# First batch of an attention and two-layer kernel: transposing the exponentials on TensorE in float32 instead of by DMA, and a new rule for VectorE or GpSimd

## The chip, the cores and the metric

One core of a Trainium2 chip. The metric is the time of one execution on the device, in microseconds; the lower, the better.

## What is computed

The input is q, k and v of 2 batches, 8 heads, 576 positions and 64 features, and the weights of two feed-forward blocks; all is float32.

```python
q_rot, k_rot = rotate(q), rotate(k)                      # rotary embedding
scores = q_rot @ k_rot^T / 8                             # per batch and head, 576 x 576
E = exp(scores - rowmax); attn = E / (rowsum(E) + 1e-9)
x = (attn @ v), heads side by side                       # 1152 tokens x 512
x = ((x @ w_a) * (x @ w_b)) @ w_out                      # 512 -> 1536 -> 512
h = x @ w_in; out = (h * tanh(softplus(h))) @ w_out2     # 512 -> 2048 -> 512
```

## The kernel before

The kernel doesn't issue instructions as it is written. Each call on an engine is recorded with a priority (`at(t)` sets it) in a `Plan`; `Plan.order` (from line 284) then places all operations with costs of its own (`Plan.cost`) and `issue` (line 376) emits them in that order, each engine's queue in order. All instructions are therefore traced at line 388, and the names of tiles tell them apart. Calls on `any_` may go to VectorE or GpSimd: GpSimd takes one if its end is at most SLACK after VectorE's, VectorE only if it ends at least BIAS earlier (lines 37 and 38).

Attention is cut into 72 units of 128 query rows (`UNITS`), 9 for each pair of heads: four row blocks for each of the two heads and one "rest" unit that holds the last 64 rows of both. Units 0 to 35 are the first batch. `attend(n)` does one:

- TensorE writes the scores into a PSUM tile s, 128x576 in two halves, with the key in two parts (qk and kl). q and k come in with the features on the partitions, and `rope` rotates them, a pair of heads ahead (products qkr and kl on `any_`, qk on ScalarE and VectorE).
- VectorE takes the negative row maximum m; ScalarE takes the exponential in place in PSUM.
- ScalarE casts it to float16 (the high part of pp), VectorE subtracts to get the low part (also pp).
- One transposing DMA on SyncE's queue turns pp (128 x 1152 float16) into pt, nine 128x128 blocks, since 576 + 576 columns are 4.5 blocks each.
- TensorE multiplies the blocks with the value parts vhl (high and low) and, for the low part of E, the shifted copy vh: 14 matmuls, into o. A first column of ones gives the row sum.
- `finish` inverts the row sums (den) and scales o into xn on VectorE for every second unit; for a rest unit into xbd. `transpose_x` brings xn and xbd onto the other axis (tile xt) with TensorE and splits it into x.

Layer 1 of the first batch (l from x and w) and layer 2 (l from ab and w) are recorded with priorities among the units of the second batch; then come layers 1 and 2 of the second batch, then the last two products (h, acc). `weights` loads a packed weight tile wr, VectorE decodes it with three integer instructions into xw, it is kept in DRAM for later (ka, ko, kc, read back as wc), ScalarE rounds it to the first part of w and an `any_` subtraction makes the second part. Layer 1 makes a_sb and ab, the latter's second part also by an `any_` subtraction. In the last stage `hidden` evaluates h into g and `accumulate` adds up acc.

PSUM holds 3 s tiles (two banks each) and 2 o tiles in the first batch, then 2 s, 2 o and 2 l.

```python
SLACK = 2000
BIAS = 2500
OFF = dict(S=-4, M=-2, E=-2, P=0, T=-1, V=4, N=-2, X=-4)   # priority offsets of a unit's steps
```

Of the kernel before, what the change touches and what calls it, by code (L numbers as in the profile page):

```python
# [9 lines left out]
F32 = mybir.dt.float32  # L10
F32R = mybir.dt.float32r
F16 = mybir.dt.float16
# [21 lines left out]
START = dict(pe=1144, sp=550)  # L34
BASE = BYTES.__array_interface__["data"][0]
TICK = 3413
SLACK = 2000
BIAS = 2500
FSLACK = 1000
FBIAS = 0  # L40
MARGIN = 0
# [129 lines left out]
class Plan:  # L171
# [88 lines left out]
    def cost(self, key, method, out, args, kw, views):  # L260

        if key == "sp":
            v = views[0]
            if method == "dma_start_transpose":
                return 1356, 1008
            return 475, int(np.prod(v.a.shape)) * v.a.itemsize / 360
        psum = any(v.root.pool.space == PSUM for v in views if v is not out)
        n = max(v.n for v in views)
        pointers = sum(v.n == 1 for v in views if v is not out) if out.n > 1 or method == "tensor_scalar" else 0
        if key == "pe":  # L270
            rhs = kw["rhs"] if method == "matmul" else args[1]
            n = rhs.n
            return n * (2 if rhs.root.dtype == F32 else 1), n * rhs.a.shape[0] / 128
        if key == "act":
            return n / 1.2 + (51 if psum else 93) + 93 * min(pointers, 1), 0
        if key == "dve":
            fast = method.startswith("tensor_scalar") or method == "tensor_copy"
            if psum:
                return n / 0.96 + 65 + 58 * min(pointers, 1), 0
            return n / (1.92 if fast else 0.96) + 69 + 58 * min(pointers, 1), 0  # L280
        if key == "pool":
            return (n * 2.132 + 132 if method != "memset" else n), 0

    def order(self):
# [17 lines left out]
        while True:  # L302
# [46 lines left out]
            if e == "sp":  # L349
                tr = op.call[1] == "dma_start_transpose"  # L350
                d0 = max(dma_free, start + (1300 if tr else 1100))
                dma_free = d0 + op.dma
                if tr:
                    free[e] = dma_free - 952
                op.end = dma_free
            else:
                op.end = free[e]
# [92 lines left out]
def kernel(ctx: ExitStack, tc: tile.TileContext, qk, v5, w1, w2, w34, tab, out):  # L450
# [13 lines left out]
    def open_pool(name, bufs=1, side="left", space=None):  # L464
        kw = dict(name=name, bufs=bufs)
        if space is not None:
            kw["space"] = space
        if space != bass.MemoryType.DRAM:
            kw.update(side=side, reuse_waits="tile")
        p = Pool(plan, space, kw)  # L470
        return p, p

    def close_pool(p):
        p.close()
# [5 lines left out]
    a0_cm, a0_p = open_pool("att0")  # L480
    d_cm, d_p = open_pool("kept", space=bass.MemoryType.DRAM)
    a_cm, a_p = open_pool("att", side="right")
    o_cm, o_ps = open_pool("o_ps", 2, side="right", space=PSUM)
    s_cm, s_ps = open_pool("s_ps", 3, space=PSUM)

    def at(t):

        plan.prio = 1000 * t
# [55 lines left out]
    xbd = [a_p.tile([128, 128], F32, tag=f"xbd{i}", name=f"xbd{i}") for i in range(2)]  # L544
    vhl = [(a_p if i < 2 else a0_p).tile([128, 5, 2, 130], F16, tag=f"vhl{i}", name=f"vhl{i}") for i in range(3)]

    vh2 = [(a_p if i < 2 else a0_p).tile([128, 4, 2, 66], F16, tag=f"vh2{i}", name=f"vh2{i}") for i in range(3)]
    vb = (0, 1, 2, 0, 1, 0, 1, 0)
    istk = ident[:, 128:192]

# [75 lines left out]
    def v_split(p):  # L626
        of = vhl[vb[p]].rearrange("p c h e -> p (c h) e")
        vt, up = v_t[p].rearrange("p (n d) -> p n d", d=D), v_up[:, p : p + 1]
        hi = of[:, :, 1 : D + 1]
        act.activation(hi, vt, AF.Copy, scale=up)  # L630
        dve.scalar_tensor_tensor(of[:, :, D + 1 : 2 * D + 1], vt, up, hi, op0=ALU.mult, op1=ALU.subtract)
        v, v2 = vhl[vb[p]], vh2[vb[p]]
        sp.dma_start(v2[0:64], v[64:128, 0:4, :, 0:66])
        sp.dma_start(v2[64:128], v[0:64, 1:5, :, 0:66])
        sp.dma_start(v[64:128, 4, :, 0 : 2 * D + 1], v[0:64, 0, :, 0 : 2 * D + 1])


    def ring_tile(n, shape, dtype, tag):
        first = n < NU // 2
        bufs = {"pp": (6, 3), "pt": (6, 4)}[tag][0 if first else 1]  # L640
        return (a0_p if first else a_p).tile(shape, dtype, tag=tag, name=f"{tag}{n}", bufs=bufs)

    o_t, xn_t, den_t = {}, {}, {}

    def attend(n):
        t0_ = t_unit(n)

        p, h, c = UNITS[n]
        tq, tk = qk_t[p]
        rest = h is None  # L650
        at(t0_ + OFF["S"])
        st = s_ps.tile([128, 2, 512], F32, tag="s", name=f"s{n}")
        for hf in range(2):
            ks = slice(HS * hf, HS * hf + HS)
            ops = []
            for i in (0, 1) if rest else (h,):
                lhsT = qz[p % 2][:, i, :] if rest else tq[i][:, 128 * c : 128 * c + 128]
                ops += [(lhsT, tk[i][:, ks]), (lhsT, kl[p % 2][i][:, ks])]
            for i, (lhsT, rhs) in enumerate(ops):
                pe.matmul(st[:, hf, :HS], lhsT=lhsT, rhs=rhs, start=(i == 0), stop=(i == len(ops) - 1))  # L660

        at(t0_ + OFF["M"])
        m = a_p.tile([128, 1], F32, tag="m", name=f"m{n}", bufs=4)
        e = st[:, :, :HS]
        dve.tensor_reduce(m, e, axis=AX.XY, op=ALU.max, negate=True)
        at(t0_ + OFF["E"])
        act.activation(e, e, AF.Exp, bias=m)
        at(t0_ + OFF["P"])
        pp = ring_tile(n, [128, 2 * S], F16, "pp")
        hi, lo = (pp[:, c : c + S].rearrange("p (a b) -> p a b", a=2) for c in (0, S))  # L670
        act.copy(hi, e)
        dve.tensor_tensor(lo, e, hi, op=ALU.subtract)
        at(t0_ + OFF["T"])
        pt = ring_tile(n, [128, 9, 128], F16, "pt")
        sp.dma_start_transpose(out=pt, in_=pp)

        at(t0_ + OFF["V"])
        vt = vhl[vb[p]]
        if rest or c % 2 == 0:
            o_t[p] = o_ps.tile([128, 512], F32, tag="o", name=f"o{n}")  # L680
        o = o_t[p]
        for i in range(9):
            for lo, w in ((0, D + 1), (D + 1, D)):
                if lo and i >= 5:
                    continue
                oc = 1 if lo else 0
                v = vt[:, i] if i < 5 else vh2[vb[p]][:, i - 5]
                if rest:
                    oo = o[:, 0:132].rearrange("p (a b) -> p a b", a=2)[:, :, oc : oc + w]
                    rhs = v[:, :, lo : lo + w]  # L690
                else:
                    base = 66 * (c % 2) + oc
                    oo = o[:, base : base + w]
                    rhs = v[:, h, lo : lo + w]
                pe.matmul(oo, lhsT=pt[:, i, :], rhs=rhs, start=(i == 0 and lo == 0), stop=(i == 8))
        if rest or c % 2:
            at(t0_ + OFF["N"])
            finish(p, rest, h, c // 2)

    def finish(p, rest, h, g):  # L700

        key = "r" if rest else h
        early = p == SPLIT
        oo = o_t[p][:, 0:132].rearrange("p (a b) -> p a b", a=2)
        den = a_p.tile([128, 2], F32, tag=f"den{key}", name=f"den{p}_{key}_{g}", bufs=2)
        dve.tensor_scalar(den, oo[:, :, 0], 1e-9, v_up[:, p : p + 1], op0=ALU.add, op1=ALU.mult)
        dve.reciprocal(den, den)
        if rest:
            for i in range(2):
                r = slice(64 * i, 64 * i + 64)  # L710
                dve.tensor_scalar_mul(xbd[p % 2][r, r], oo[r, i, 1 : D + 1], den[r, i : i + 1])
            return
        part = early and g
        if (p, part) not in xn_t:
            xp = a0_p if p in (0, 2) or early else a_p
            n = 2 if early else 4
            xn_t[p, part] = xp.tile([128, 4, 2, D], F32, tag="xn", name=f"xn{p}_{g}", bufs=2 if xp is a0_p else 1)[:, 0:n]
        c = 0 if early else 2 * g
        dve.tensor_tensor(
            xn_t[p, part][:, c : c + 2, h, :], oo[:, :, 1 : D + 1], den.unsqueeze(2).to_broadcast([128, 2, D]), op=ALU.mult  # L720
        )

# [142 lines left out]
        pool.memset(xbd[i], 0.0)  # L865
    for i in range(3):
        pool.memset(vhl[i][:, :, :, 0:1], 1.0)
    at(0)

    t = o_ps.tile([128, 512], F32, tag="o", name="warm")  # L870
# [29 lines left out]
    for n in range(NU):  # L900
        p, h, c = UNITS[n]
        if n == NU // 2:
            close_pool(s_cm)
            l_cm, l_ps = open_pool("l_ps", 2, space=PSUM)
            s_cm, s_ps = open_pool("s_ps2", 2, space=PSUM)
        if n == NU // 2 + 2:
            close_pool(a0_cm)
            ab_cm, ab_p = open_pool("ab")
        attend(n)
        if n == V_AT:  # L910
            at(t_unit(n) + VP[2])
            for i in range(1, NP):
# [37 lines left out]
    T = layer1(0, T, DT * G, F0)  # L950
    y0 = layer2(0, T, DT * G, between2)
    T += 24 * DT * G
    close_pool(s_cm)
    close_pool(o_cm)
    close_pool(a_cm)
# [158 lines left out]
```

## Time and profile before

| | us |
|---|---|
| runs, median of 3 | 645.03 (642.63 to 646.7) |
| the profiled execution, whole | 647.88 |
| its span, first to last instruction | 646.1 |
| TensorE busy | 573.7 |
| VectorE busy | 391.8 |
| GpSimd busy | 324.7 |
| ScalarE busy | 309.4 |

PE is TensorE's matmuls, PEld its weight loads, DVE VectorE, ACT ScalarE, POOL GpSimd, SP SyncE. In the stretches, PEclk is the granted TensorE clock as a share of 2.4 GHz: 0.50 is the lower level, 1.2 GHz. A wait is told as who waited, for whom, in total, how often, and the longest.

### The profile page before, as it was taken

The numbers are of one execution on the slowest core, as the hardware profiler recorded it, in microseconds if no ns is written. First come the engines' busy times: TensorE is split into PE (matmuls) and PEld (weight loads), VectorE is DVE, ScalarE is ACT, GpSimd is POOL, SyncE is SP. The second block draws the span as 40 slices with busy tenths as digits, with TensorE's granted clock in tenths as the row PEclk, the third lists the DMA queues.
The fourth block names the chain that finished last, engine by engine and source line by source line (L and its number), as shares of the span: only waits on it lengthen the run. The fifth ranks groups of instructions, "written<-read, shape, count | busy, mean of one in ns | idle before, by whom it ended". The sixth has DMA issues, their size and how long they took to land.

```text
span 646.1 us, 11253 instructions
## 1 busy us (share of the span) xinstructions
PE 573.7 (89%) x4168; PEld 523.6 (81%) x4168; DVE 391.8 (61%) x687; ACT 309.4 (48%) x583; POOL 324.7 (50%) x261
## 2 busy tenths in 40 slices
PE   6575656699899888899999999999999999999997
PEld 5564545589788777788999999997888899899885
DVE  6979768979688877889668999971101112111111
ACT  4957646557465564444344444226443345343230
POOL 5460753465853763423489787557444443332120
PEclk7676767779899988999999999999999999999999
DMA  8496997977878986999799788974333324220002
GB/s 290 87 201 166 218 238 149 209 209 210 200 161 204 274 183 174 230 304 271 209 399 329 238 282 281 293 280 138 112 97 96 89 92 138 80 79 17 1 1 82
DMA packets 135127, 118.13 MB, mean 183 GB/s; under 512 B 99232, under 2 KB 100896, under 8 KB 135072
## 3 DMA queue, kind: packets, MB, share of 16 engines
q1 hardware_dynamic: 135072, 117.41, 66.6%
q8 instruction: 33, 0.54, 0.3%
q14 instruction: 22, 0.18, 0.1%
HBM read 74.61 MB, written 20.19 MB: 147 GB/s over the span
## 4 chain that ended last, share of the span: by engine, by line
PE 67%; DMA 19%; DVE 8%; ACT 3%; issue 2%; SPq 1%; POOL 0%; DVEq 0%; ACTq 0%; POOLq 0%
PE l L388 28%; DMA pt<-pp 16%; PE acc L388 16%; PE h L388 15%; PE o L388 5%; PE s L388 3%; DVE pp L388 2%; DMA wr<-in_w_dram 2%; DVE m L388 1%; DVE xw L388 1%; SPq L388 1%; DMA qkr_k<-in_qk_dram 1%; DVE qk L388 1%; ACT qk L388 1%; PE xt L388 1%
## 5 line engine op out<-in xcount | busy, mean ns | idle before, releaser
L388 POOL TENSOR_TENSOR w<-wc,w 128x512 fp32r<-128x512 f32 x100 | 135.8, 1361 | 146.6 <-ACT w L388 125.5
L388 PE MATMUL l<-x,w 128*128 128x320 f32 (+1 forms) x1152 | 172.9, 305 | 1.5 <-ACT w L388 1.0
L388 PEld LDWEIGHTS l<-x,w 128*128 128x128 f32 x1152 | 161.0, 195 | 2.5 <-ACT w L388 1.5
L388 DVE SCALAR_TENSOR_TENSOR xw<-wr,xw 128x512 uint32<-128x512 uint32 x136 | 128.2, 959 | 0.1
L388 DVE TENSOR_TENSOR g<-h,g 128x320 fp32r<-128x320 f32 (+1 forms) x48 | 26.8, 558 | 155.6 <-ACT g L388 155.6
L388 PE MATMUL acc<-w,g 128*128 128x512 f32 x432 | 105.7, 396 | 0.6 <-ACT g L388 0.6
L388 PE MATMUL h<-y,w 128*128 128x320 f32 (+1 forms) x576 | 104.8, 336 | 0.2 <-DVE g L388 0.2
L388 PEld LDWEIGHTS h<-y,w 128*128 128x128 f32 x576 | 93.5, 188 | 9.7 <-DVE g L388 0.5
L388 ACT CAST w<-wc 128x512 fp32r<-128x512 f32 x100 | 61.4, 619 | 80.7 <-PE l L388 24.5
L388 PEld LDWEIGHTS acc<-w,g 128*128 128x128 f32 x432 | 80.6, 188 | 19.0 <-ACT g L388 1.0
L388 PEld LDWEIGHTS <-pt 128*128 128x128 f16 x1008 | 47.0, 110 | 49.3 <-DMA pt<-pp 41.6
L388 POOL TENSOR_TENSOR w<-xw,w 128x512 fp32r<-128x512 f32 x36 | 49.5, 1378 | 68.0 <-ACT w L388 62.9
L388 PE MATMUL l<-ab,w 128*128 128x256 f32 (+1 forms) x576 | 81.8, 298 | 1.7 <-ACT w L388 1.5
L388 PEld LDWEIGHTS l<-ab,w 128*128 128x128 f32 x576 | 77.5, 190 | 2.9 <-ACT w L388 2.3
L388 PE MATMUL o<-vhl,pt 128*128 128x65 f16 (+1 forms) x720 | 46.4, 216 | 37.4 <-DMA pt<-pp 33.9
L388 ACT ACTIVATE s<-s,m 128x576 f32<-128x576 f32 x72 | 50.8, 715 | 46.8 <-DVE m L388 42.7
L388 POOL TENSOR_TENSOR ab<-a_sb,ab 128x256 fp32r<-128x256 f32 (+1 forms) x48 | 50.7, 1060 | 27.9 <-ACT ab L388 20.1
L388 POOL TENSOR_TENSOR qkr<-qkr,cs 128x576 f32<-128x576 f32 x28 | 41.8, 1510 | 42.6 <-DMA qkr<-in_qk_dram 42.6
L388 PE MATMUL s<-qk 128*128 128x288 f32 x128 | 45.8, 370 | 18.1 <-DVE pp L388 13.2
L388 DVE TENSOR_TENSOR pp<-s,pp 128x576 f16<-128x576 f32 x72 | 53.5, 749 | 11.1 <-ACT pp L388 10.6
L388 DVE TENSOR_SCALAR xw<-wr 128x512 uint32<-128x512 uint32 x68 | 51.7, 774 | 10.0 <-DMA wr<-in_w_dram 8.5
L388 DVE TENSOR_REDUCE m<-s 128x1 f32<-128x576 f32 x72 | 53.1, 749 | 5.3 <-PE s L388 5.0
(73 smaller groups left out, 578.7 us busy)
## 6 DMA issues: line engine op xcount, KB each, us to landing
wr<-in_w_dram SPq DMA_DIRECT2D x68, 512.0 KB, 5.1
wc<-kc SPq DMA_DIRECT2D x64, 256.0 KB, 2.7
kc<-xw SPq DMA_DIRECT2D x32, 256.0 KB, 3.3
qkr<-in_qk_dram SPq DMA_DIRECT2D x14, 576.0 KB, 5.4
ka<-xw SPq DMA_DIRECT2D x24, 256.0 KB, 2.7
wc<-ka SPq DMA_DIRECT2D x24, 256.0 KB, 5.8
ko<-xw SPq DMA_DIRECT2D x12, 256.0 KB, 3.1
wc<-ko SPq DMA_DIRECT2D x12, 256.0 KB, 3.7
```

The lines of the kernel that those rows point to most:

```text
L388: getattr(engine, method)(*map(real, args), **{k: real(v) for k, v in kw.items()})
```

## The change

In the first batch `attend0` takes the place of `attend`. The exponential goes from PSUM to an SBUF tile e (float32, one for two units). TensorE transposes four blocks of 128x128 of each unit into PSUM (tile tm, 512 columns), and for a pair of units their last 128 columns into tile tr (256 columns, 128 for a rest unit). ScalarE casts the transposed PSUM tile to float16 (the high part) and VectorE subtracts (the low part), into ptm and ptr. The fifth block overlaps the fourth, so its value tile vr has zeros in the upper half; all parts use the same value tiles, 15 matmuls a unit. `finish` copies o to SBUF (ob) on ScalarE in the first batch, and scales it into xn on `any_`. PSUM holds 2 s, 1 o, 2 tm and 1 tr in the first batch, then 2 s, 2 o and 2 l. SLACK and BIAS become 0, so that an `any_` operation goes to the engine that would end it first. The planner's costs of a DMA and three offsets of priorities differ too.

```diff
-SLACK = 2000
-BIAS = 2500
+SLACK = 0
+BIAS = 0
...
-                return 1356, 1008
-            return 475, int(np.prod(v.a.shape)) * v.a.itemsize / 360
+                return 1356, 1700
+            return 475, int(np.prod(v.a.shape)) * v.a.itemsize / 320
...
-                    free[e] = dma_free - 952
+                    free[e] = max(free[e], dma_free - 1700)
...
-OFF = dict(S=-4, M=-2, E=-2, P=0, T=-1, V=4, N=-2, X=-4)
+OFF = dict(S=-8, M=-8, E=-8, P=0, T=-1, V=4, N=-2, X=-4)
...
-    o_cm, o_ps = open_pool("o_ps", 2, side="right", space=PSUM)
-    s_cm, s_ps = open_pool("s_ps", 3, space=PSUM)
+    o_cm, o_ps = open_pool("o_ps", 1, side="right", space=PSUM)
+    s_cm, s_ps = open_pool("s_ps", 2, side="right", space=PSUM)
+    t_cm, t_ps = open_pool("t_ps", 1, space=PSUM)
...
+        if p < NP:
+            pool.tensor_copy(vr[vb[p]][64:128, :, 0 : 2 * D + 1], v[64:128, 4, :, 0 : 2 * D + 1])
+            return
...
+    def attend0(n):
...
+        s, m = scores(n)
+        if not j:
+            e_t[0] = a0_p.tile([128, 2, S], F32, tag="e", name=f"e{n}", bufs=3)
+        e = e_t[0]
+        act.activation(e[:, j, :].rearrange("p (a b) -> p a b", a=2), s, AF.Exp, bias=m)
+
+        def parts(x, name, bufs):
+            w = 128 * len(x)
+            at(t0_ + OFF["T"])
+            t = t_ps.tile([128, w], F32, tag=name, name=f"{name}{n}", bufs=bufs)
+            for i, b in enumerate(x):
+                pe.transpose(t[:, 128 * i : 128 * i + 128], b, ident[:, 0:128])
+            at(t0_ + OFF["P"])
+            pt = a0_p.tile([128, 2, w], F16, tag=f"p{name}", name=f"p{name}{n}", bufs=6)
+            act.copy(pt[:, 0, :], t)
+            dve.tensor_tensor(pt[:, 1, :], t, pt[:, 0, :], op=ALU.subtract)
+            return pt
+
+        pt_t[j] = parts([e[:, j, 128 * i : 128 * i + 128] for i in range(4)], "tm", 2)
+        if not (rest or j):
+            return
+        pr = parts([e[:, i, S - 128 :] for i in range(1 + j)], "tr", 1)
+        for i in (0,) if rest else (0, 1):
+            chunks = [(*(pt_t[i][:, q, 128 * k : 128 * k + 128] for q in (0, 1)), vhl[vb[p]][:, k]) for k in range(4)]
+            chunks.append((*(pr[:, q, 128 * i : 128 * i + 128] for q in (0, 1)), vr[vb[p]]))
+            weighted(n if rest else n - 1 + i, chunks)
...
+        if p < NP:
+            ob = a0_p.tile([128, 2, 66], F32, tag="ob", name=f"ob{p}_{key}_{g}", bufs=3)
+            act.copy(ob[:, :, 0 : D + 1], oo[:, :, 0 : D + 1])
+            oo, eng = ob, any_
...
-        attend(n)
+        (attend0 if n < NU // 2 else attend)(n)
```

How the order of the instructions moves is seen at two places. The first is TensorE's queue in the first batch, after scores of the second pair of heads. Before, the output matmuls of a unit (o, here of a rest unit) stand between scores, and each needs the block pt that a DMA brings:

```order
L388 MATMUL s_413<-kl_98,qk_229 128x288
L388 MATMUL s_427<-qk_229 128x288
L388 MATMUL vs_434<-ident,v_mx 3x128
L388 MATMUL s_427<-kl_98,qk_229 128x288
L388 MATMUL s_427<-qk_229 128x288
L388 MATMUL s_427<-kl_98,qk_229 128x288
L388 LDWEIGHTS pt_345
L388 MATMUL o_444<-vhl_128,pt_345 128x2x65
```

Now, in the first pair of heads, transposes of e into tm and tr stand between the scores, and the output matmuls take their weights from ptm and ptr:

```order
L388 MATMUL s_313<-kl_95,qk_169 128x288
L388 MATMUL tm_311<-ident,e_262 128x128 x3
L388 MATMUL tr_328<-ident,e_262 128x128 x2
L388 LDWEIGHTS ptm_257
L388 MATMUL o_338<-vhl_131,ptm_257 128x65
L388 MATMUL tm_340<-ident,e_302 128x128 x4
L388 MATMUL s_347<-qk_169 128x288
L388 MATMUL s_347<-kl_95,qk_169 128x288
```

No instruction of that queue waits for a transposing DMA any more until the second batch; it waits for ScalarE and VectorE instead. The second place is VectorE's queue in the second batch, where weights are decoded (xw) between the maxima (m) and the subtractions (pp) of the units. Before:

```order
L388 SCALAR_TENSOR_TENSOR xw_2698<-wr_2456,xw_2698 128x512
L388 SCALAR_TENSOR_TENSOR xw_2711<-wr_2573,xw_2711 128x512
L388 TENSOR_SCALAR den_1_0_2759<-o_2704,v_up 128x2
L388 TENSOR_TENSOR pp_2706<-s_2653,pp_2706 128x576
L388 RECIPROCAL den_1_0_2759<-den_1_0_2759 128x2
L388 TENSOR_REDUCE m_2774<-s_2683 128x1
```

Now, at the same kind of place:

```order
L388 SCALAR_TENSOR_TENSOR xw_3030<-wr_2737,xw_3030 128x512
L388 TENSOR_REDUCE m_3057<-s_3047 128x1
L388 SCALAR_TENSOR_TENSOR xw_3054<-wr_2868,xw_3054 128x512
L388 TENSOR_TENSOR w_3059<-xw_3030,w_3059 128x512
L388 SCALAR_TENSOR_TENSOR xw_3054<-wr_2868,xw_3054 128x512
L388 TENSOR_TENSOR pp_2963<-s_2898,pp_2963 128x576
L388 TENSOR_SCALAR xw_3086<-wr_2955 128x512
L388 TENSOR_TENSOR w_3079<-xw_3054,w_3079 128x512
```

The subtractions that make the second part of w have come over from GpSimd's queue into VectorE's, among the work of the units.

## Rows read from the trace of the kernel before

**Rows 1.** The page: TensorE's busy time, and the chain by engine and by line.
```profile
PE 573.7 (89%) x4168; PEld 523.6 (81%) x4168; DVE 391.8 (61%) x687; ACT 309.4 (48%) x583; POOL 324.7 (50%) x261
...
PE 67%; DMA 19%; DVE 8%; ACT 3%; issue 2%; SPq 1%; POOL 0%; DVEq 0%; ACTq 0%; POOLq 0%
PE l L388 28%; DMA pt<-pp 16%; PE acc L388 16%; PE h L388 15%; PE o L388 5%; PE s L388 3%; DVE pp L388 2%; DMA wr<-in_w_dram 2%; DVE m L388 1%; DVE xw L388 1%; SPq L388 1%; DMA qkr_k<-in_qk_dram 1%; DVE qk L388 1%; ACT qk L388 1%; PE xt L388 1%
```

**Rows 2.** The maxima m (first and last start); busy time in A, B, C, D.
```profile
L388 DVE TENSOR_REDUCE m<-s x72: 731/748/760, 15.0 to 304.9; 128x1 f32<-128x576 f32 x72
...
core 0: us, PE busy (x) PEld busy (x) DVE busy (x) ACT busy (x) POOL busy (x), PEclk, DMA share, GB/s
...
15.00:136.30 121.30, 76.82 (x716) 67.16 (x717) 97.96 (x197) 75.74 (x127) 58.09 (x40) 0.68 0.87 186
136.30:304.90 168.60, 150.49 (x1366) 140.50 (x1365) 142.54 (x279) 95.67 (x176) 88.80 (x70) 0.97 0.86 218
304.90:440.00 135.10, 135.03 (x1043) 134.55 (x1042) 111.34 (x142) 50.83 (x107) 94.27 (x73) 1.00 0.84 280
440.00:646.10 206.10, 201.53 (x1009) 173.15 (x1007) 30.67 (x54) 80.67 (x161) 76.31 (x60) 1.00 0.27 79
```

**Rows 3.** The chain in order of time: start, us, what; two pieces.
```profile
105.42 0.95 PE o L388 x14
...
317.65 122.40 PE l L388 x916
```

**Rows 4.** TensorE's waits in A: who for whom, us, times, longest.
```profile
PE o L388 <- DMA pt<-pp: 20.6, 17, 3.0
PE s L388 <- DVE pp L388: 12.2, 7, 3.0
```

**Rows 5.** The same in B.
```profile
PE o L388 <- DMA pt<-pp: 13.3, 10, 3.0
```

**Rows 6.** VectorE's timeline near 286 us: start, us, instruction.
```profile
285.92 0.75 DVE L388 TENSOR_TENSOR pp<-s,pp 128x576 f16<-128x576 f32 x1
286.58 0.48 DVE L388 TENSOR_TENSOR y<-l,y 128x320 fp32r<-128x320 f32 x1
```

**Rows 7.** VectorE's groups by shape: times, busy us, mean ns, idle before.
```profile
L388 DVE TENSOR_TENSOR g<-h,g 128x512 fp32r<-128x512 f32 x16 | 11.1, 692 | 66.2 <-ACT g L388 66.2
L388 DVE TENSOR_TENSOR a_sb<-a_sb,l 128x256 f32<-128x256 f32 x24 | 9.9, 414 | 5.6 <-PE l L388 5.5
...
L388 DVE TENSOR_TENSOR xn<-o,den 128x128 f32<-128x128 f32 x32 | 9.0, 281 | 0.0
```

**Rows 8.** Busy time by stretch: VectorE's fullest 50 us.
```profile
350.00:400.00 50.00, 50.00 (x378) 50.00 (x377) 45.98 (x53) 21.48 (x47) 39.90 (x32) 1.00 0.84 275
```

**Rows 9.** Two xt transposes in TensorE's timeline, and the stretch around them.
```profile
174.58 0.63 PE L388 MATMUL xt<-ident,xn 128*128 128x128 f32 x2
175.00 0.53 PE L388 MATMUL xt<-ident,xbd 128*128 128x64 f32 x2
...
174.50:175.20 0.70, 0.70 (x5) 0.70 (x4) 0.00 (x0) 0.00 (x0) 0.70 (x1) 0.50 0.49 105
```

**Rows 10.** VectorE on tiles xw and pp: ns min/median/max; then xw's group (mean ns).
```profile
L388 DVE SCALAR_TENSOR_TENSOR xw<-wr,xw x136: 662/685/1837, 64.0 to 432.4; 128x512 uint32<-128x512 uint32 x136
L388 DVE TENSOR_SCALAR xw<-wr x68: 404/427/1895, 63.0 to 427.7; 128x512 uint32<-128x512 uint32 x68
...
L388 DVE TENSOR_TENSOR pp<-s,pp x72: 730/748/760, 19.7 to 309.2; 128x576 f16<-128x576 f32 x72
...
L388 DVE SCALAR_TENSOR_TENSOR xw<-wr,xw 128x512 uint32<-128x512 uint32 x136 | 128.2, 959 | 0.1
```

**Rows 11.** GpSimd's groups by shape in B.
```profile
L388 POOL TENSOR_TENSOR w<-xw,w 128x512 fp32r<-128x512 f32 x27 | 36.8, 1363 | 47.9 <-ACT w L388 42.8 <-PE o L388 4.3 <-POOL kl L388 0.7
L388 POOL TENSOR_TENSOR ab<-a_sb,ab 128x320 fp32r<-128x320 f32 x12 | 13.6, 1134 | 10.5 <-ACT ab L388 9.5 <-PE l L388 0.8
L388 POOL TENSOR_TENSOR qkr<-qkr,cs 128x576 f32<-128x576 f32 x8 | 12.1, 1521 | 0.8 <-DMA qkr<-in_qk_dram 0.8
```

More of the change, by code (lines that the diff above doesn't have):

```diff
@@ L482 @@
     a_cm, a_p = open_pool("att", side="right")
-    o_cm, o_ps = open_pool("o_ps", 2, side="right", space=PSUM)
-    s_cm, s_ps = open_pool("s_ps", 3, space=PSUM)
+    o_cm, o_ps = open_pool("o_ps", 1, side="right", space=PSUM)
+    s_cm, s_ps = open_pool("s_ps", 2, side="right", space=PSUM)
+    t_cm, t_ps = open_pool("t_ps", 1, space=PSUM)
+    o2_ps = None
     def at(t):
@@ L545 @@
     vhl = [(a_p if i < 2 else a0_p).tile([128, 5, 2, 130], F16, tag=f"vhl{i}", name=f"vhl{i}") for i in range(3)]
-    vh2 = [(a_p if i < 2 else a0_p).tile([128, 4, 2, 66], F16, tag=f"vh2{i}", name=f"vh2{i}") for i in range(3)]
+    vh2 = [a_p.tile([128, 4, 2, 66], F16, tag=f"vh2{i}", name=f"vh2{i}") for i in range(2)]
+    vr = [a0_p.tile([128, 2, 130], F16, tag=f"vr{i}", name=f"vr{i}") for i in range(3)]
     vb = (0, 1, 2, 0, 1, 0, 1, 0)
@@ L631, in v_split @@
         dve.scalar_tensor_tensor(of[:, :, D + 1 : 2 * D + 1], vt, up, hi, op0=ALU.mult, op1=ALU.subtract)
-        v, v2 = vhl[vb[p]], vh2[vb[p]]
+        v = vhl[vb[p]]
+        if p < NP:
+            pool.tensor_copy(vr[vb[p]][64:128, :, 0 : 2 * D + 1], v[64:128, 4, :, 0 : 2 * D + 1])
+            return
+        v2 = vh2[vb[p]]
         sp.dma_start(v2[0:64], v[64:128, 0:4, :, 0:66])
@@ L635, in v_split, with scores @@
         sp.dma_start(v[64:128, 4, :, 0 : 2 * D + 1], v[0:64, 0, :, 0 : 2 * D + 1])
[L638 to L641, printed above, removed]
     o_t, xn_t, den_t = {}, {}, {}
-    def attend(n):
+    def scores(n):
         t0_ = t_unit(n)
@@ L666, in attend, with weighted @@
         at(t0_ + OFF["E"])
+        return e, m
+    def weighted(n, chunks):
+        p, h, c = UNITS[n]
+        rest = h is None
+        at(t_unit(n) + OFF["V"])
+        if rest or c % 2 == 0:
+            o_t[p] = (o2_ps if o2_ps and n % 2 else o_ps).tile([128, 512], F32, tag="o", name=f"o{n}")
+        o = o_t[p]
+        ops = [(x, v, lo, w) for x, l, v in chunks for lo, w in ((0, D + 1), (D + 1, D)) if x is not None]
+        ops += [(x, v, 0, D + 1) for l, x, v in chunks if x is not None]
+        for i, (x, v, lo, w) in enumerate(ops):
+            oc = 1 if lo else 0
+            if rest:
+                oo = o[:, 0:132].rearrange("p (a b) -> p a b", a=2)[:, :, oc : oc + w]
+                rhs = v[:, :, lo : lo + w]
+            else:
+                base = 66 * (c % 2) + oc
+                oo = o[:, base : base + w]
+                rhs = v[:, h, lo : lo + w]
+            pe.matmul(oo, lhsT=x, rhs=rhs, start=(i == 0), stop=(i == len(ops) - 1))
+        if rest or c % 2:
+            at(t_unit(n) + OFF["N"])
+            finish(p, rest, h, c // 2)
@@ new lines @@
+    e_t, pt_t = {}, {}
+    def attend0(n):
+        p, h, c = UNITS[n]
+        rest = h is None
+        t0_ = t_unit(n)
+        j = 0 if rest else c % 2
+        s, m = scores(n)
[22 more added lines that the diff above has]
+            weighted(n if rest else n - 1 + i, chunks)
@@ L667, in attend @@
+    def attend(n):
+        p = UNITS[n][0]
+        t0_ = t_unit(n)
+        e, m = scores(n)
         act.activation(e, e, AF.Exp, bias=m)
         at(t0_ + OFF["P"])
-        pp = ring_tile(n, [128, 2 * S], F16, "pp")
+        pp = a_p.tile([128, 2 * S], F16, tag="pp", name=f"pp{n}", bufs=3)
         hi, lo = (pp[:, c : c + S].rearrange("p (a b) -> p a b", a=2) for c in (0, S))
@@ L673, in attend @@
         at(t0_ + OFF["T"])
-        pt = ring_tile(n, [128, 9, 128], F16, "pt")
+        pt = a_p.tile([128, 9, 128], F16, tag="pt", name=f"pt{n}", bufs=4)
         sp.dma_start_transpose(out=pt, in_=pp)
[L677 to L698, printed above, removed]
+        v, v2 = vhl[vb[p]], vh2[vb[p]]
+        weighted(n, [(pt[:, i], None, v[:, i]) for i in range(5)] + [(None, pt[:, i + 5], v2[:, i]) for i in range(4)])
     def finish(p, rest, h, g):
@@ L703, in finish @@
         early = p == SPLIT
-        oo = o_t[p][:, 0:132].rearrange("p (a b) -> p a b", a=2)
+        oo, eng = o_t[p][:, 0:132].rearrange("p (a b) -> p a b", a=2), dve
+        if p < NP:
+            ob = a0_p.tile([128, 2, 66], F32, tag="ob", name=f"ob{p}_{key}_{g}", bufs=3)
+            act.copy(ob[:, :, 0 : D + 1], oo[:, :, 0 : D + 1])
+            oo, eng = ob, any_
         den = a_p.tile([128, 2], F32, tag=f"den{key}", name=f"den{p}_{key}_{g}", bufs=2)
@@ L718, in finish @@
         c = 0 if early else 2 * g
-        dve.tensor_tensor(
+        eng.tensor_tensor(
             xn_t[p, part][:, c : c + 2, h, :], oo[:, :, 1 : D + 1], den.unsqueeze(2).to_broadcast([128, 2, D]), op=ALU.mult
@@ L867 @@
         pool.memset(vhl[i][:, :, :, 0:1], 1.0)
+        pool.memset(vr[i][0:64], 0.0)
     at(0)
@@ L902 @@
         if n == NU // 2:
-            close_pool(s_cm)
+            close_pool(t_cm)
             l_cm, l_ps = open_pool("l_ps", 2, space=PSUM)
-            s_cm, s_ps = open_pool("s_ps2", 2, space=PSUM)
+            o2_cm, o2_ps = open_pool("o2_ps", 1, space=PSUM)
         if n == NU // 2 + 2:
@@ L952 @@
     T += 24 * DT * G
+    close_pool(o2_cm)
     close_pool(s_cm)
```

## The prediction

> **What bounds the kernel now.** I read the page first, then the stretches between the points where the work changes, then the waits in each stretch, and last the durations that the sum needs.
>
> The page gives TensorE 89% of the span as busy and two thirds of the chain that ended last; most of the rest of that chain is DMA, and nearly all of that is the transposing DMA from pp to pt [rows 1]. The stretches [rows 2] tell where. I cut them at the row maxima (m): the 1st of the 72 begins at 15.0 us, the last at 304.9 [rows 2], and the 37th, first of the second batch, at 136.3, where the stretch is cut. So A is the first batch's attention (121.3 us), B the second batch's with layer 1 of the first batch in between (168.6), C the two layers up to 440, D the last two products. In C and D TensorE is full, at a granted clock of 1.00: 916 matmuls of layers 1 and 2 take 122.4 us without a break, 0.134 us each [rows 3]. There only fewer matmuls help. In A TensorE is busy 63% of the time at 0.68, the DMA engines 0.87, VectorE 81%. In A TensorE waits 20.6 us for transposing DMAs, and 12.2 us to write scores into an s buffer that VectorE still reads for pp [rows 4]. In B all three are at 85 to 90%, and 13.3 us of waiting for pt are left [rows 5]. So A has room; B has little.
>
> **The change, part by part.**
>
> *What goes in A.* All 36 transposing DMAs of the first batch, both waits of [rows 4] with them: an s buffer is now free after the exponential, which writes to an e tile in SBUF. This cover gone, what is late next is whichever engine carries most in A.
>
> *VectorE in A.* Back to back, a VectorE instruction occupies about 0.07 us less than its row says: a pp of 0.75 us starts at 285.92 and the next at 286.58 [rows 6]. So 36 pp subtractions go, 36 x 0.67 = 24.1 us. In their place stand 36 subtractions of 128x512 from PSUM; the g subtraction of that size takes 0.692 [rows 7], less 0.07 is 0.62, 22.3 us; and 16 of 128x256 and 4 of 128x128, by the a_sb row of 0.414 and one step lower (0.28) 0.34 and 0.21, 6.3 us. Five rope products and one kl come from GpSimd by the new tie rule (+4.0), 8 xn products go there (-1.6), and two weights are decoded later (each a TENSOR_SCALAR of 0.43 and two SCALAR_TENSOR_TENSOR of 0.685 [rows 10], 1.6 less the overlap, so -3.2). Sum +3.7; GpSimd, which also loses its weights here, holds VectorE up less (below), some 4 us. VectorE carries 98 us in A before [rows 2] and 98 after. The gain in A is therefore only what VectorE stood still: 121.3 - 98 = 23 us at most. In its fullest 50 us it reached 46.0, 92% [rows 8]. I take that: 98 / 0.92 = 106.5 us, 14.8 saved. Bounds: 101 us at 97%, 121 us at today's 81%.
>
> *TensorE in A* gets 180 transposes. Two xt transposes of the same 128x128 float32 shape begin 0.42 us apart from what follows, 0.21 us each, while the clock was granted at 0.50 [rows 9], that is 1.2 GHz; at 2.4 GHz I estimate half. So 19 to 38 us, 31 at A's mean clock of 0.68; there are 36 more short matmuls for the outputs (15 a unit, not 14) at 0.95 / 14 = 0.07 [rows 3], 2.5 us, and 23 layer 1 matmuls stand later, 5 us. At that clock the sum is 76.8 + 31 + 2.5 - 5 = 105, all of A. In B, where TensorE stands still less, the granted clock was 0.97 [rows 2]; at that one the sum is 105 x 0.68 / 0.97 = 74. I take a value between, 85 to 90 us, which VectorE covers; if the clock stays where it is, TensorE is the bound of A itself, at about 112 us.
> The Trainium skill (FP8 and Floating Point Precision, section TensorE Precision Notes) says that true float32 takes four passes through the array; by that I estimate 0.43 us for a transpose at 1.2 GHz. The xt row, 0.21, is half of it, so the sum doesn't use the rule; the time by it is rival 4.
>
> *ScalarE in A* loses 36 casts of 128x576 and gains 36 of 128x512, 20 smaller ones and 20 copies of o, some 12 us on 75.7 [rows 2]: 88 of 106, hidden behind VectorE.
>
> *SyncE's queue in A* also loses the 8 copies to vh and 4 to vhl that made the value parts for pt's odd blocks; 4 short GpSimd copies (vr) replace them. I cost that at nothing: GpSimd has half of A free.
>
> *The tie rule.* VectorE now takes 132 of 136 weight subtractions (w) and 42 of 48 ab ones from GpSimd. In B these are 24 w at 0.62 (14.9 us, by the g row) and 18 ab of 128x256 or 128x320 at about 0.37 (6.7, by the a_sb row of 0.414 and the y row of 0.48, less 0.07) [rows 6, 7]. Behind each of them wait, in VectorE's order, the maxima and pp of the next units, so they are on the path. Against that: xw's row runs from 0.66 to 1.84 us, with a median of 0.685 and a mean of 0.959 [rows 10], which I read as waiting for GpSimd. All of B's VectorE instructions at their shortest durations, less the overlap, come to 122 us; measured are 142.5, so 20.5 us are such waiting, over 97 instructions that read SBUF alone (0.21 each). GpSimd has 88.8 us of work in B now and loses 24 of 27 w at 1.36 and 18 of 24 ab at about 1 [rows 11], down to about 38. With 142 such instructions after, 20.5 x 142/97 x 38/88.8 = 13 us. VectorE in B: 142.5 + 21.6 - 7.5 = 157 us. TensorE there loses 17 layer 1 matmuls and 28 short ones, 4 us of 150.5. The order after places the output matmuls of B later behind their DMAs and the scores earlier, so most of the 13.3 us should go; then VectorE is the bound, and with its order written to fit I take 95 to 96%: 164 us, 5 less than now. Bounds: 157 if it never waits, 185 at the 85% of today.
> The Trainium skill (SBUF — State Buffer, Who interferes with whom) says that a VectorE instruction with two SBUF inputs blocks, and is blocked by, a GpSimd instruction that reads SBUF, for the whole instruction. The xw row agrees, and so does pp, which reads one operand from PSUM and stays between 0.730 and 0.760 [rows 10]. The rule speaks against the moved subtractions, which have two SBUF inputs too; what that costs is in the 13 us above and in rival 1.
>
> *C and D.* Up to the 72nd scores 689 layer matmuls are done and not 729, and 28 fewer output matmuls: 40 x 0.134 + 28 x 0.07 = 7.3 us move behind. VectorE in C goes from 111 to about 114 us of 135 [rows 2]: 37 us of weight subtractions, 11 of ab and 4 more for decoding come, and the waiting for GpSimd, which has 94 us of work there now, goes. TensorE stays full: 341.2 + 7.3 = 348.5.
>
> **Sum.** 15 + 106.5 + 164 + 348.5 = 634 us against a span of 646.1, 12 less. The profiled execution took 647.9 and the runs' median is 645.0, so I set 645.0 - 12 = **633 us**.
>
> **Rivals.**
> 1. *VectorE is overloaded in B* (slower). The 142 instructions wait as long for GpSimd as before, 0.21 us each, since the rope products that GpSimd keeps are the long ones (1.5 us): 144 + 30 = 174 us, at 95% 183. Then 15 + 106.5 + 183 + 348.5 = 653, a run of 652. It decides from B = 176 on, that is VectorE at 167 us. For it: all new work in B is on the engine that waits least. Against: GpSimd is then busy a fifth of the time, not half.
> 2. *The DMA hid VectorE* (no change). If the 81% in A is what dependences allow, A stays at 121: 649, a run of 648. For it: VectorE's load in A is the same, and TensorE and ScalarE come close to it. Against: the waits of [rows 4] go entirely.
> 3. *Everything fits.* A at 97% (101 us) and B at 157: 15 + 101 + 157 + 348.5 = 621.5, a run of 620. For it: TensorE's clock rises and VectorE's long xw disappear.
> 4. *TensorE is the bound of A* (slower). A transpose takes twice the xt row's 0.21 us, so 76 us, and the clock stays at 0.68: 76.8 + 76 + 2.5 - 5 = 150 us for A, 677 in all, a run of 676. Against: the row.
> That the change doesn't do what it says is ruled out by the order, which holds 36 transposing DMAs instead of 72.
>
> **How the numbers follow.** My forecast, A between 103 and 112 with B between 158 and 170, has 0.45 and spans 622 to 645. Rival 3 has 0.18, rival 2 0.20, rival 1 0.15, rival 4 0.02. A measurement here tells about 1% from no change: below 638.6 is faster, above 651.5 slower. Faster: 0.36 of the forecast, rival 3, 0.03 of rival 2, so 0.57. Slower: rivals 1 and 4, 0.17. The rest, 0.26, is no change. The range takes in rivals 1 to 3 with a few us on either side: 617 to 655.
>
> **What would show it.** After: the 37th m near 121 us, the 72nd near 286, and 348 us from there; tm transposes near 0.11 to 0.21 us. Wrong if A's waits are TensorE's own (transposes near 0.43 us, clock at 0.50); if xw stays at a mean of 0.95 us; if TensorE has gaps after the 72nd m that end on DVE w; or if the first 36 maxima need 121 us again. A time above 651 with B longer than 176 is rival 1; one below 622 with VectorE near 97% is rival 3.

## The result and the profile after

The changed kernel takes 635.5 us (median of 4 runs, 634.5 to 636.1) against 645.9 of the kernel before (4 runs): a ratio of 0.9846, 95% interval 0.9806 to 0.9886. It is faster by 1.5%, and the whole interval lies below 1. The forecast was 633. The profiled execution took 635.9, its span 634.2.

The page of the changed kernel, its busy times and its chain by engine and by line, to be held against [rows 1]:

```profile
PE 580.2 (91%) x4384; PEld 529.3 (83%) x4384; DVE 457.5 (72%) x882; ACT 314.6 (50%) x623; POOL 90.7 (14%) x93
...
PE 64%; DVE 26%; issue 3%; ACT 3%; DMA 3%; SPq 1%; DVEq 0%
PE l L388 27%; PE acc L388 16%; PE h L388 15%; DVE xw L388 5%; DVE m L388 5%; DVE ptm L388 3%; PE s L388 3%; DVE w L388 2%; PE o L388 2%; DVE pp L388 1%; DVE den L388 1%; DVE qk L388 1%; ACT w L388 1%; DVE vhl L388 1%; DMA wr<-in_w_dram 1%
```

The transposing DMA, 16% of the chain before, is no longer among its lines, and VectorE has gone from 8% to 26%. Next the maxima m, and the busy time between the 1st, the 37th and the 72nd of them (A, B, and C with D in one row; columns as in [rows 2]):

```profile
L388 DVE TENSOR_REDUCE m<-s x72: 716/746/759, 15.3 to 284.6; 128x1 f32<-128x576 f32 x72
...
15.30:114.70 99.40, 78.42 (x910) 68.57 (x911) 97.79 (x207) 76.73 (x157) 40.39 (x37) 0.93 0.26 81
114.70:284.65 169.95, 148.70 (x1316) 138.77 (x1315) 164.81 (x320) 95.19 (x177) 41.17 (x30) 0.95 0.87 218
284.65:634.20 349.55, 344.45 (x2120) 314.55 (x2119) 185.27 (x341) 135.24 (x274) 1.32 (x4) 1.00 0.51 163
```

A is 99.4 us instead of 121.3, with VectorE busy 97.8 of them, 98%. B is 169.9 instead of 168.6, and VectorE carries 164.8 there, 97%, where it was 142.5. C and D take 349.6 instead of 341.2. So 22 us won in A, 1 lost in B, 8 in C and D. The waits say the same. TensorE's in A (who for whom, us, times, longest), against [rows 4]:

```profile
PE o L388 <- DVE ptr L388: 4.1, 4, 2.4
PE tm L388 <- DVE ptm L388: 4.1, 8, 1.4
PE o L388 <- ACT ob L388: 3.0, 3, 1.6
PE tm L388 <- ACT e L388: 2.4, 1, 2.4
```

and all that VectorE waits for in A:

```profile
DVE m L388 <- PE s L388: 0.6, 2, 0.4
DVE ptr L388 <- ACT ptr L388: 0.2, 1, 0.2
```

TensorE waits in many small pieces, for VectorE (10 us over all its rows) and ScalarE (11) about alike, while VectorE hardly stands idle: the bound of A is VectorE. Not all of its 97.8 busy us are work, though; what some of its records hold besides is in the last section.

### The profile page after: what moved, and what is told of

Read it like the earlier page. It is cut to its first block, busy times and chain, and to the rows that moved or that the text cites. A ratio compares the mean times of both kernels' runs of the same rounds, so it can differ in the third digit from the quotient of the medians.

```text
span 634.2 us, 11508 instructions
## 1 busy us (share of the span) xinstructions
PE 580.2 (91%) x4384; PEld 529.3 (83%) x4384; DVE 457.5 (72%) x882; ACT 314.6 (50%) x623; POOL 90.7 (14%) x93
## 4 chain that ended last, share of the span: by engine, by line
PE 64%; DVE 26%; issue 3%; ACT 3%; DMA 3%; SPq 1%; DVEq 0%
PE l L388 27%; PE acc L388 16%; PE h L388 15%; DVE xw L388 5%; DVE m L388 5%; DVE ptm L388 3%; PE s L388 3%; DVE w L388 2%; PE o L388 2%; DVE pp L388 1%; DVE den L388 1%; DVE qk L388 1%; ACT w L388 1%; DVE vhl L388 1%; DMA wr<-in_w_dram 1%
## 5 line engine op out<-in xcount | busy, mean ns | idle before, releaser
L388 DVE TENSOR_TENSOR w<-wc,w 128x512 fp32r<-128x512 f32 x100 | 68.5, 690 | 103.6 <-ACT w L388 103.2
L388 DVE SCALAR_TENSOR_TENSOR xw<-wr,xw 128x512 uint32<-128x512 uint32 x136 | 97.9, 723 | 1.3
L388 PE MATMUL l<-ab,w 128*128 128x320 f32 (+1 forms) x576 | 82.6, 299 | 3.2 <-ACT w L388 2.8
L388 ACT ACTIVATE h<-h 128x320 f32<-128x320 f32 (+1 forms) x48 | 22.8, 476 | 59.8 <-PE h L388 59.8
L388 ACT ACTIVATE s<-s,m 128x576 f32<-128x576 f32 x36 | 25.5, 714 | 30.5 <-DVE m L388 26.8
L388 PE MATMUL s<-kl,qk 128*128 128x288 f32 x128 | 38.2, 313 | 1.1 <-DVE kl L388 1.1
L388 PEld LDWEIGHTS s<-qk 128*128 128x128 f32 x128 | 25.7, 202 | 13.7 <-DVE qk L388 3.2
L388 ACT CAST w<-xw 128x512 fp32r<-128x512 f32 x36 | 22.3, 620 | 28.9 <-DVE xw L388 28.7
L388 ACT CAST ab<-a_sb 128x256 fp32r<-128x256 f32 (+1 forms) x48 | 20.7, 432 | 25.4 <-DVE a_sb L388 25.0
L388 PE MATMUL tm<-ident,e 128*128 128x128 f32 x144 | 26.0, 289 | 7.3 <-DVE ptm L388 4.1
```

The source lines that it names most:

```text
L388: getattr(engine, method)(*map(real, args), **{k: real(v) for k, v in kw.items()})
```

## The experiments

The change has three parts that can be made apart: the transposes on TensorE (T), the tie rule (R: SLACK and BIAS 0), and the planner's numbers (C: the costs of a DMA and the three offsets). Their edits are these lines of the diff:

```diff
R -SLACK = 2000; BIAS = 2500
R +SLACK = 0; BIAS = 0
C -return 1356, 1008        ... itemsize / 360        free[e] = dma_free - 952
C +return 1356, 1700        ... itemsize / 320        free[e] = max(free[e], dma_free - 1700)
C -OFF = dict(S=-4, M=-2, E=-2, ...)
C +OFF = dict(S=-8, M=-8, E=-8, ...)
```

All eight combinations were run (ratio to the kernel before, 95% interval; median us):

| | without T | with T |
|---|---|---|
| neither | 1 (645 to 646) | 0.9927 [0.9889, 0.9964], 640.4 |
| R | 1.0057 [1.0038, 1.0076], 649.6 | 1.0208 [1.0151, 1.0266], 659.4 |
| C | 0.9849 [0.9813, 0.9885], 636.3 | 0.9798 [0.9778, 0.9818], 632.7 |
| R and C | 0.993 [0.9894, 0.9966], 641.1 | 0.9846 [0.9806, 0.9886], 635.5: the change |

**C alone** (the kernel before with the C lines).

> The kernel before with the planner's new DMA costs and the three new offsets alone. Theory V: 641 to 648, as before within 1%, with the waits for pt in B shorter than 13 us if the costs fit better. Rival C (the order written with truer costs is what gains): 633 to 638.

Measured 636.3 us, ratio 0.9849: the whole of the change's gain, with none of its transposes. Its stretch A, and what TensorE waits for there:

```profile
16.62:117.32 100.70, 68.73 (x636) 60.62 (x637) 91.73 (x180) 71.19 (x119) 51.09 (x36) 0.67 0.90 182
...
PE s L388 <- DVE pp L388: 11.7, 10, 2.5
PE o L388 <- ACT vhl L388: 4.0, 2, 2.6
```

All 36 transposing DMAs are still there (DMA share 0.90, as 0.87 before), the granted clock is still 0.67, and yet A is 100.7 us. A part of that is the cut, since 56 output matmuls of the last four units and 24 of the 26 of layer 1 have moved behind it; but the sum of the stretches, the time, is that of the changed kernel. Of the 20.6 us of waiting for pt in A nothing is left, of the 13.3 in B 2.5, though over all 72 such a DMA takes about as long from issue to landing as before (the last line of tile pt, min/median/max, before and in this run):

```profile
DMA to landing us min/median/max: 3.2/4.2/7.9
```

```profile
DMA to landing us min/median/max: 3.2/3.9/8.9
```

What changed most is where the output matmuls stand: far enough behind their DMA that it has landed. In the traces, with each DMA paired with its unit's first output weights, those of the first batch begin 7.5 us after the issue (median), before 5.8, and of the 36 only one begins within 0.3 us of the landing, before 17. The 36 DMAs themselves land after 3.4 us instead of 4.3 (medians), so a smaller part is theirs. In the chain DMA falls from 19% to 6%.

**The tie rule alone, and undone in the change.**

> The kernel before with the new tie rule alone (SLACK 0, BIAS 0). Theory V: A stays at 118 to 122 us, since the transposing DMAs hold it, and B, where VectorE gains work, is 168 to 175: a run of 644 to 652. Rival R: VectorE's long xw disappear and the run takes 632 to 638.

> The changed kernel with the old tie rule (SLACK 2000, BIAS 2500): all weight and ab subtractions and the rope stay on GpSimd. Theory V (the gain is the transposing DMAs that left A; A is now as long as VectorE's work there, and the tie rule only swaps VectorE's work for its waiting): A 98 to 105 us instead of 99.4, B 164 to 170 instead of 170 with VectorE's load down from 165 to about 145, a run of 632 to 640. Rival R (the gain comes from VectorE no longer waiting for GpSimd): A grows back past 110 us, a run of 643 or more.

Alone it makes the kernel before slower, 649.6 us, but not in A: that was to stay at 118 to 122 us and is shorter by 9, with 15.1 us of waiting for pt left in it:

```profile
16.85:129.10 112.25, 77.57 (x718) 66.15 (x719) 102.92 (x209) 73.36 (x123) 42.17 (x29) 0.70 0.95 196
```

Against that, A starts 1.9 us later and B is longer. Undone in the change, the time is 632.7 instead of 635.5; these two intervals just overlap, but R has the same sign in all four pairs of the table (0.6% alone, 0.8% beside C, 2.8% beside T, 0.5% beside both). Stretch B of the two runs, R alone first:

```profile
129.10:307.69 178.59, 154.83 (x1372) 145.24 (x1371) 162.86 (x321) 95.71 (x176) 37.87 (x28) 0.94 0.82 209
```

```profile
115.44:275.32 159.88, 144.22 (x1275) 133.35 (x1274) 144.47 (x270) 94.42 (x176) 96.06 (x74) 0.95 0.91 228
```

With the rule VectorE carries 163 to 165 us in B, without it 142 to 144, and B is longer by 10 us in either pair (168.6 to 178.6; 159.9 to 169.9). In the change 7 of the 10 come back in C and D (356.4 without the rule, 349.6 with it). Beside T without C the loss lies elsewhere: in A VectorE's load rises from 97.7 to 113.8 us, and A from 104.1 to 123.1 (the rows are in the next two parts).

**The transposes alone** (the changed kernel with the R and C lines of before).

> The kernel before with the transposes on TensorE alone: old tie rule, old DMA costs, old offsets. Rival V (taking the transposing DMAs out of A is what shortens it): A 100 to 106, a run of 628 to 640. Theory O: without the lead the transposes add a step for which TensorE waits and shorten nothing: A 115 us or more, a run of 645 to 658.

Measured 640.4 us, a ratio of 0.9927, between the two expectations. A and B, and TensorE's longest wait in A:

```profile
14.75:118.84 104.09, 78.07 (x822) 68.19 (x822) 97.69 (x181) 78.93 (x156) 64.68 (x57) 0.90 0.30 100
118.84:300.15 181.31, 159.24 (x1483) 148.69 (x1483) 153.85 (x300) 99.68 (x187) 92.01 (x74) 0.96 0.84 205
...
PE tm L388 <- ACT e L388: 14.4, 20, 2.3
```

A falls to 104.1 us, but B rises to 181.3 and C and D are 343.1: 75 output matmuls of the last units and the 26 of layer 1 now stand behind A (B holds 1483 matmuls, before 1366), and TensorE waits 14.4 us in A for the exponential, where transposes stand right behind the scores. The profile is of the slowest run, 645.0 us, so one or more of these stretches are longer than in the others, by some 4.6 us together; where isn't known. By the times, an A shorter by 17 us is worth 5 here.

**Without the planner's numbers** (the changed kernel with the C lines of before), and **with the old offsets alone** (only the OFF line of before).

> The changed kernel with the planner's old DMA costs and old offsets; transposes on TensorE and the new tie rule stay. Theory V: A 98 to 103 us as in the changed kernel, B 168 to 175, a run of 633 to 640. Rival C: the gain is gone, 643 or more.

> The changed kernel with the three old offsets; the new DMA costs stay. Theory O: TensorE waits for ScalarE's exponential before its transposes as with all old costs (12 us in A), a run of 648 to 662. Theory D: 633 to 640.

Measured 659.4 us, slower than the kernel before (1.0208), and 642.9 (0.9962, interval 0.9927 to 0.9997). So in the changed kernel the new offsets are worth some 7 us (642.9 to 635.5) and the new costs of a DMA 16 more (659.4 to 642.9). The time with only the offsets of before lies between the two expectations. The waits tell a part of what each does. With all C lines of before, A, then TensorE's longest wait there and its longest in B:

```profile
16.70:139.78 123.08, 93.06 (x895) 81.87 (x896) 113.79 (x219) 81.82 (x162) 42.95 (x36) 0.81 0.27 86
...
PE tm L388 <- ACT e L388: 12.1, 13, 2.7
...
PE o L388 <- DMA pt<-pp: 12.4, 14, 2.6
```

With only the offsets of before, the first wait in A is about the same and that in B is not among its rows:

```profile
14.93:129.51 114.58, 85.38 (x896) 75.13 (x896) 111.34 (x220) 82.11 (x162) 39.18 (x34) 0.86 0.29 93
...
PE tm L388 <- ACT e L388: 13.3, 18, 2.4
```

The offsets bring scores, maximum and exponential of a unit earlier, so that a transpose finds its exponential done: A goes from 114.6 to 99.4 us, and C and D give 7 of that back. The costs place the second batch's output matmuls behind the landing of their DMA, which shortens B by 5 us (174.2 to 169.5). The greater part of their gain, 8.5 us (123.1 to 114.6), lies in A, where no transposing DMA is left and the wait for the exponential stays. Why stays open: the costs are three numbers, two for the transposing DMA and one for all others, and were not changed one by one.

**The offsets alone, in the kernel before.**

> The kernel before with the three new offsets alone (scores, maximum and exponential of a unit at -8; DMA costs as before). Theory O (the greater lead of scores, maxima and exponentials over the rest of a unit is what empties VectorE's gaps in A): VectorE in A above 88%, A 100 to 106 us, a run of 633 to 640. Theory D (the truer DMA costs in the order are what counts): as before, 642 to 648.

Measured 642.4 us, 0.9958 (0.9922 to 0.9993): less than a third of C. A is 107.4 us, but 14.3 us of waiting for pt stay in A and 9.1 in B. The rest of C's gain needs the costs of a DMA.

**R and C without T.**

> The changed kernel without its transposes: the kernel before with the new tie rule, DMA costs and offsets. It shows what the transposes are worth within the change. If they are worth what they were with the old tie rule (5 us): a run of 638 to 643. Rival V (the transposing DMAs hold A): A back near 121 us, 650 or more. If the transposes are worth nothing: 633 to 637.

Measured 641.1 us (0.993). Its profile is of its slowest run, 648.1 us, so only the times are used. Against it, the transposes are worth 5.5 us in the full change.

**More work for VectorE** (each maximum of the first batch is taken twice; nobody reads the second).

```diff
+        m2 = a_p.tile([128, 1], F32, tag="mm", name=f"mm{n}", bufs=4)
+        dve.tensor_reduce(m2, s, axis=AX.XY, op=ALU.max, negate=True)
```

> The changed kernel with each row maximum of the first batch taken twice, the second into a tile that nobody reads: 36 x 0.67 = 24 us more for VectorE in A and nothing else. If VectorE sets the length of A: A 118 to 126 us, a run of 655 to 663. If something else does (TensorE, ScalarE, the PSUM tiles): less than 8 us more, 636 to 643.

Measured 665.3 us; A is 124.2 us:

```profile
15.37:139.57 124.20, 88.14 (x928) 77.72 (x929) 116.81 (x239) 79.34 (x159) 44.51 (x44) 0.87 0.21 69
```

36 x 0.67 = 24 us of work lengthen A by 24.8 us, with TensorE busy only 71% of it. VectorE's busy time itself rises by 19.0 us, since some of its other records are shorter here, and it is busy 94% of A. So A is VectorE's, if not to the last microsecond.

**More work for TensorE** (every transpose is made twice).

```diff
+            for _ in range(2):
-            for i, b in enumerate(x):
-                pe.transpose(t[:, 128 * i : 128 * i + 128], b, ident[:, 0:128])
+                for i, b in enumerate(x):
+                    pe.transpose(t[:, 128 * i : 128 * i + 128], b, ident[:, 0:128])
```

> The changed kernel with every transpose of the first batch done twice into the same place: 180 more, 20 us for TensorE at 2.4 GHz. If TensorE's work in A lies beside VectorE's (78 of 99 us busy now): less than 10 us more, 636 to 645. If TensorE bounds A as much as VectorE does: 20 us more, 652 or more.

Measured 646.4 us, 11 more than the change: neither "beside" nor "bound". A in that run:

```profile
15.55:121.36 105.81, 94.12 (x1073) 86.80 (x1071) 103.65 (x208) 79.76 (x160) 42.46 (x37) 0.95 0.28 91
```

A has 6.4 us more, and VectorE is still busy 98% of it; its load has risen by 5.9 us with one instruction more, though the edit gives it no work. By the trace, about half of that is other work, since the order written anew puts two more kl, one more qk and qkr and two more xw into A for some shorter ones; the other half, 2.9 us, is records that GpSimd holds up (the last section). TensorE, at 89%, is close behind. How much of the 11 us is TensorE's own stays open.

**The tie rule for the rope and xn products only**, and **a longer lead** (old tie rule, offsets -12).

```diff
+slack, bias = (2000, 2500) if kind == "any" and op.big else (SLACK, BIAS) ...   # op.big: tiles w and ab
```

```diff
-SLACK = 0; BIAS = 0; OFF = dict(S=-8, M=-8, E=-8, ...)
+SLACK = 2000; BIAS = 2500; OFF = dict(S=-12, M=-12, E=-12, ...)
```

> The changed kernel with the old tie rule for the weight and ab subtractions, the new one for the rope products and xn. If it is the moved weight and ab work that costs in B: B 158 to 164 us with VectorE's load near 145, a run of 631 to 634, as with the old tie rule everywhere. If the rope's moves matter: away from that by more than 4 us.

> The changed kernel with the old tie rule and the three offsets at -12 instead of -8. If more lead still fills gaps: a run of 625 to 631. If VectorE and the buffers leave no more to fill: 631 to 636.

Measured 636.0 us (0.984, 0.9792 to 0.9889) and 631.5 us (0.9765, 0.9725 to 0.9805). With w and ab on GpSimd again, B falls to 162.3 us, but C and D take 357.7, and the time is that of the change: what B gains is handed on. Which of R's decisions cost its 0.5% stays open, being of the size of the intervals. The second is the fastest kernel of the study, 2.3% below the kernel before, and its interval ends just where that of the change begins: the best version keeps the transposes and the planner's numbers, with a longer lead, and leaves the tie rule as it was. What the lead of 12 adds to that of 8 (632.7) is inside the intervals; A is 92.2 us instead of 100.7, but B 168.8 instead of 159.9.

## Why the prediction was right, and where it was not

**The time and the sign** were right: 633 forecast, 635.5 measured, and neither of the slower rivals came about. That the time came so close is in part luck. The stretches show errors that cancel: A 99.4 us (forecast 106.5, its band 103 to 112), B 169.9 (164), C and D 349.6 (348.5). And one part of the change, priced at nothing in A, gives the whole gain without the others.

**"So A has room" and "What goes in A".** The step that failed is the cause: it puts the room in A down to the transposing DMAs, which only the transposes would take away, and costs the planner's numbers at nothing in A. Either opens that room: A is 104.1 us with T alone and 100.7 with C alone, and C without T has the change's time. The waits for pt of [rows 4] were in the main waits of a place in a queue (an output matmul 1.7 us too near to the issue of its DMA, by the medians above), not of a DMA that was too slow. The transposes gain 4 to 6 us where C is there (636.3 to 632.7 without R, with intervals that just overlap, 641.1 to 635.5 with it), and without C, beside R, they lose 10 (649.6 to 659.4). For B the prediction had the step (the order "after places the output matmuls of B later"), and it held: no wait for pt is left in B's rows. It was not drawn out to A, nor were the offsets priced at all.

**VectorE in A** was right in its load (98 forecast, 97.8 measured) and in being the bound, which the second maximum shows. The term that was mis-sized is the share of time that it works: 92% was taken from its fullest stretch before, 98% came, and A ended below the lower bound of 101 us. (The overlap of 0.07 us in that sum is 0.09 by its own row, 0.75 less 0.66; with about as many instructions gone as come, that moves it by about 1 us.) The 4 us that GpSimd was to hold VectorE up less in A did not come, 7.4 us before and 8.8 after by records (counted as under the tie rule below), so the load came out right by a miss elsewhere in the sum, which stays open.

**TensorE in A** was right: covered, 78.4 us of work against 85 to 90 forecast, and the granted clock rose to 0.93, with TensorE busy 79% of A instead of 63%. In the runs with transposes it is 0.81 to 0.96 in A, in those without 0.67 to 0.74; what of the change raises it was not tried by itself. ScalarE's 88 us came to 76.7, and nothing hung on it. The transposes came as the xt row said. TensorE's timeline, an early piece at a granted clock of 0.50 and a later one at 1.00 (start, us, instruction):

```profile
16.89 0.90 PE L388 MATMUL tm<-ident,e 128*128 128x128 f32 x3 [2.43 <-ACT e L388]
...
23.80 0.60 PE L388 MATMUL tm<-ident,e 128*128 128x128 f32 x4
```

Alone such a matmul has a record of 0.27 us (its median), so four in 0.60 begin (0.60 - 0.27) / 3 = 0.11 us apart; the three in 0.90, with records of 0.47 (the longest), 0.21 apart. These are the two prices of the sum, and rival 4, which wanted twice the 0.21, fell with them. By the rule of four passes for true float32 (the Trainium skill, FP8 and Floating Point Precision, TensorE Precision Notes) I estimate 0.43 at the lower level; the trace, with 0.21, doesn't agree for these transposes.

**The tie rule in B** was right in kind and too small in size. Forecast were 24 w and 18 ab for 21.6 us and VectorE at 157 us; it carried 164.8. Its groups in B (busy us, mean ns):

```profile
L388 DVE SCALAR_TENSOR_TENSOR xw<-wr,xw 128x512 uint32<-128x512 uint32 x59 | 44.0, 753 | 0.1
...
L388 DVE TENSOR_TENSOR w<-xw,w 128x512 fp32r<-128x512 f32 x24 | 20.3, 850 | 0.0
...
L388 DVE TENSOR_TENSOR ab<-a_sb,ab 128x320 fp32r<-128x320 f32 x10 | 6.7, 672 | 0.0
...
L388 DVE TENSOR_TENSOR ab<-a_sb,ab 128x256 fp32r<-128x256 f32 x8 | 4.5, 565 | 0.0
```

The counts are those of the forecast, 24 and 18. They take 20.3 + 6.7 + 4.5 = 31.5, less 42 x 0.07 for the overlap 28.6 us: 7 more than their price in the sum. The w of C and D, where GpSimd has 1.3 us of work, take 0.690 on the mean (the page's group of 100); beside a GpSimd busy a quarter of B they take 0.850. So the moved subtractions wait as well, and the trace shows which: 17 of the 24 w overlap no GpSimd instruction and take 0.68 on the mean; five w and three ab that begin while one runs take 0.9 to 1.9, 7.2 us more in all. The term that was mis-sized is the waiting for GpSimd. It was to fall with GpSimd's work, from 20.5 us to 13; by the prediction's own measure, 164.8 less the 144 of rival 1, it is 21, which is the miss. Counted by records (those more than 0.08 us above the median of their like that overlap no GpSimd instruction) it is 13.8 us before and 16.9 after. The mean of xw fell as forecast, from 0.96 to 0.72 over the whole run. Rival 1's mechanism was at work, not quite half of the way from 157 to its 174, and short of the 167 from which it was to decide.

**C and D** came as computed: 7.3 us more forecast, 8.3 measured, from 68 matmuls that stand later (2052 before, 2120 after).

## What to carry to other kernels

Before a wait for a DMA is removed by moving its work to an engine, see whether the waiter only stands too close behind the issue: here a planner's prices of a DMA (for the transposing one 1.7 us instead of 1.0) and a lead of a few units gave what a new path for half of the work was credited with. Numbers that set the order are edits of their own and want a price and a run of their own; of three parts made together, one can pay for another's loss. Where an order is written anew with every edit, a stretch's length is read with what lies in it, since work that leaves a stretch comes back in a later one.

## What was not expected of the hardware

With o copied from PSUM to SBUF (ob), to free the one o tile early, the small VectorE instructions after it came out slower. In A of the changed kernel, reading the copy (busy us, mean ns):

```profile
L388 DVE TENSOR_SCALAR den<-ob,v_up 128x2 f32<-128x2 f32 x16 | 6.2, 390 | 0.1
L388 DVE TENSOR_SCALAR xbd<-ob_r,den_r 64x64 f32<-64x64 f32 x8 | 3.9, 494 | 0.1
L388 DVE TENSOR_TENSOR xn<-ob,den 128x128 f32<-128x128 f32 x7 | 3.8, 537 | 0.0
```

and in B of the same kernel, where the second batch still reads o in PSUM:

```profile
L388 DVE TENSOR_TENSOR xn<-o,den 128x128 f32<-128x128 f32 x14 | 3.9, 279 | 0.0
...
L388 DVE TENSOR_SCALAR den<-o,v_up 128x2 f32<-128x2 f32 x14 | 3.0, 211 | 0.3 <-PE o L388 0.3
...
L388 DVE TENSOR_SCALAR xbd<-o,den_r 64x64 f32<-64x64 f32 x6 | 1.7, 282 | 0.1
```

By these means 16 x 0.18 + 8 x 0.21 + 7 x 0.26 = 6 us of VectorE in the stretch that it bounds, while GpSimd is busy 40% of it. The trace shows that the copy by itself isn't slow to read. Of the 16 den on ob, 12 overlap no GpSimd instruction and take 0.22 us on the mean, as from PSUM; three of the others take 1.0 to 1.2. Reading o in PSUM, 13 of the 32 den of the kernel before overlap one too, and none takes over 0.222. The longest den, and the GpSimd instruction that runs when it begins (start, us, instruction):

```profile
49.36 1.24 DVE L388 TENSOR_SCALAR den<-ob,v_up 128x2 f32<-128x2 f32 x1
```

```profile
49.17 1.41 POOL L388 TENSOR_TENSOR qkr<-qkr 128x576 f32<-128x576 f32 x1
```

The one ends at 50.60, the other at 50.58. So it is with every record over 0.35 us of these tiles (den, xbd, xn) in A: it ends 0.02 to 0.15 us after the GpSimd instruction under which it began, and in B the w ones end 0.55 after it. In A of the changed kernel these waits, with those of xw, qk and qkr, come to 8.8 of VectorE's 97.8 busy us; in C and D, where GpSimd has 1.3 us of work, there is none. The Trainium skill (SBUF — State Buffer, Who interferes with whom) says that a VectorE instruction with two SBUF inputs and a GpSimd one that reads SBUF shut each other out; the xn rows agree, 0.279 with one operand in PSUM and 0.537 with both in SBUF.
